# One fused block on one Trainium2 core: the same ramp, another hand-written order from the first value products on, the gate row for w_out among the first output projections, the last output tile in two parts

## The chip, the core and the metric

The kernel runs on one core of a Trainium2 chip. A core has five engines that each run their own list of instructions in order: TensorE (PE, matrix products, with PEld for the loading of weights), VectorE (DVE), ScalarE (ACT), GpSimd (POOL) and SyncE (SP, which only issues DMAs here). They meet through semaphores. The metric is device time in microseconds (us) of one execution; times of a kernel are given as the median of several runs.

## What is computed

x has S = 2048 rows and D = 448 columns, in bf16. Cut to what matters:

```python
mod = (silu(c) @ w_mod)                      # six vectors sa, ca, ga, sb, cb, gb
h = layernorm(x) * (1 + ca) + sa
q, k, v = split(h @ wqkv)                    # 16 heads of 28
phi(u) = concat(softmax(u @ w_phi), softmax(-u @ w_phi))
kv, z = phi(k)^T v, sum(phi(k))              # per head
x = x + ga * ((phi(q) kv / (phi(q) z)) @ wo)
h = layernorm(x) * (1 + cb) + sb
z = gelu(h @ w_in)                           # 2048 x 1792
z1, z2 = z[:, :896], layernorm(z[:, 896:])
g = w_sp @ z2 + b_sp                         # w_sp is 2048 x 2048
x = x + gb * ((z1 * g) @ w_out)
```

## The kernel before

The rows are cut into 16 tiles of 128. All weights and activations stay in SBUF; modulation is folded into the weights (SC and SH steps scale and shift them, so that the layer norm's scale and offset cost nothing per tile), and the gates ga and gb are folded into wo and w_out (gr and ge make a gate row with one product and one copy, wos and wts multiply it in).

Everything is written as small steps, and one string, `ORDER`, names the steps in the order in which they are emitted. A word is `step:arguments@bank/engine`. A loop at the end of `fast_path` runs over the words; each engine gets its instructions in this order, and no scheduler moves them (`tc.manual_schedule()`). The letter behind the slash says which engine does the step: V is VectorE, S ScalarE, G GpSimd, Y SyncE. The part behind the @ is the PSUM space: A0, A1 and A2 have two banks each, B0 and B1 one bank each. A step that takes a space waits until what stood there has been read. So the order of the words sets the order on every engine, and where two engines must meet.

The steps of which this text speaks, by place in the program:

- Start: `consts` (L682) fills constants, f_zero among them; `du` (L726) are dummy products of f_zero that fill PE ahead of the first data; `ld` (L679) issues a load; `l1s`, `l1e`, `l1r`, `l1a` (L855 to L867) are the first layer norm, `l1a` its last step per tile; `X` (L877) transposes the first tiles on PE, `T1` (L872) the others two at a time with a DMA on SP.
- Attention, first half: `EPq` (L796) folds w_phi into the q weights; `kM`, `vM`, `qM` (L890, L898, L945) are the products for k, v and q; `kE` and `kF` (L893) the exponentials of plus and minus k on ScalarE, `vC` (L901) the copy of v, `kS`, `kR`, `kP` (L904 to L911) sums, reciprocals and products that make the softmax; `kA` (L921) adds a tile to kv. `qE` and `qF` (L950) are the exponentials of q.
- Attention, second half: `nM` (L973) numerator and denominator, `nX`, `nC`, `nS`, `nT` (L977 to L989) the division, `T2` (SP) a transpose, `wM` (L1003, L1005) the output projection into x_ps, `wR` and `wQ` (L1010, L1012, L1017) the residual add and the square for the second layer norm, `l2R`, `l2r`, `l2a` the rest of it. `nA` and `l2a` write tiles for the transposes `T2` and `T3`.
- gMLP: `SCw` (L796, L798, L800) scales w_in; `zM` (L1049) is the second half of h @ w_in, `zG` (L1053) its gelu on ScalarE, `zQ`, `zR`, `zW`, `zN` its layer norm, which ends in the tile z2n (L1072); `yM` and `yG` (L1078, L1081) are the first half.
- Spatial product: `W` (L1086) are transposing loads of pieces of w_sp on SP, into the buffers f_wsp, f_Eq and f_hT; the last two are buffers of earlier stages, and so such a load waits until the earlier stage has read them. The product is arranged in blocks with seven products in place of eight: `gM` (L1145) is one plain column of blocks, `P` (L1124) the others, `d` and `x` (L1133, L1140) their sums and the product with z1, `tT` (L1102) and `sS` (L1109) sums of tiles of z2n and of w_sp.
- Output: `oM` (L1159), `oE` (L1162), `oD` (L1165): seven matmuls, the eviction with the residual add, and the store of one tile.

`general_path` is a fallback that a flag starts; it does not run here.

Of the kernel before, what the change touches and what calls it, by code (L numbers as in the profile page):

```python
# [481 lines left out]
ORDER = """tbl du:8@B1 m2b/V ld:wk/Y du:3@A2 m2a/V du:11@A1 ld:c/Y ct@B0 ld:x1/S l1s:1 ld:x0/S l1s:0 m1/G ld:phi/Y ce:1 m3 FTk:1@B1 ce:2 l1e:1,2/G ld:wsa/Y du:2@A0  # L482
l1e:0,1/G FTk:0@A0 ld:wca/Y ce:3 ce:4 bd/V ld:x2/Y ld:wq/Y l1r:0,1 l1a:0/V du:6@A2 X:0@B0 ETk:0/S csA@A2 ETk:1/V PFk:2@B1 l1r:1,2 esA l1a:1/G X:1@A0 XE:0/V
m4 du:2@A2 FSk@B0 ccA@A1 FCk/S PFk:0@B0 ecA XE:1/S EPk:0/V EPk:2/S l1s:3 du:1@A2 PFk:1@A1 EPk:1/S ld:wv/Y l1s:2 PFk:3@A0 l1e:2,4/V EPk:3/S du:2@B0 kM:1@B1
FTq:1@A2 ETq:1/V ld:x3/Y FTq:0@B0 ETq:0/V kM:0@A0 kF:1 FSq@A2 FCq/V kE:1 kS:1 PFq:1@B0 scb kF:0 kE:0 l1r:2,4 l1a:2/G l1a:3/G l1s:4 X:2@B1 SHv@A1 PFq:2@A2
# [4 lines left out]
qF:0 kS:5 vC:6 kM:6@A2 l1a:10/G kS:4 vC:5 l1a:11/G qM:2@A1 kF:6 kR:5 kF:7 kR:4 kE:6 kP:5/V ld:wcb/Y qF:2 T1:8,10 kP:4/V kS:6 kR:6 vM:7@B1 kE:7 T1:10,12  # L490
kA:3@A0 wos:0/G l1e:12,16/G vM:4@A2 l1r:12,16 vC:7 qE:2 l1a:15/G kM:9@B0 kF:9 l1a:12/V l1a:14/G kM:8@B1 l1a:13/V vM:9@A1 kE:9 kS:7 kR:7 kF:8 vC:4 kS:9
kE:8 kS:8 T1:12,14 kM:10@B0 kP:6/G kE:10 kP:7/G kR:8 kF:10 kA:4@A0 kA:5@A0 kM:11@B1 kE:11 T1:14,16 kS:10 vM:10@B0 kF:11 kS:11 kA:6@A0 vC:9 kA:7@A0 kM:12@B1
kP:8/G kR:10 kE:12 kR:9 kP:9/V kR:11 vC:10 kP:10/V kF:12 kS:12 kM:13@A1 kR:12 vM:8@A2 kM:15@B0 vC:8 kF:13 kP:11/G kM:14@B1 ld:wsb/Y kE:13 kS:13 kR:13 kE:14
W:0,6 kF:14 kE:15 kA:8@A0 kA:9@A0 kP:12/V kS:14 vM:11@A1 kF:15 kS:15 kA:10@A0 vM:14@B1 kR:14 vC:11 vM:15@B0 vC:14 vM:12@A2 vM:13@B1 vC:12 kA:11@A0 vC:13
kP:13/G kA:12@A0 kR:15 kP:14/V kP:15/V wos:2/V kA:13@A0 kA:14@A0 vC:15 kA:15@A0 KV:0/V KV:1/V KZ:0 ld:win0/S qM:3@A2 KZ:1 nM:0@A1 qE:3 ld:wout/S nM:1@A0
nX:0 nX:1 qF:3 nC:0 csB@B0 W:0,1 ld:win1/Y nC:1 nS:0 ccB@B1 nT:0 qM:4@A2 qE:4 nA:0/V nT:1 ecB nA:1/V wos:3/V qM:5@A1 nM:2@A0 qF:4 esB nX:2 nM:3@A2 nX:3
FB@B1 wos:1/V nC:2 qE:5 T2:0,1 nC:3 nS:1 FBc/S qF:5 nT:2 nA:2/G wM:0/S@B0 nT:3 SHw:3@B1 wR:0/S SCw:0,3/S T2:1,2 nM:5@A1 nX:5 nM:4@A0 nC:5 nX:4 nC:4 nA:3/V
wQ:0/S wM:1/S@B0 wR:1/S SHw:2@B1 SCw:2,1/S qM:6@A2 SCw:0,0/S SCw:3,1/G nS:2 nT:5 nT:4 T2:2,4 nM:6@A1 wQ:1/V qE:6 nX:6 nM:7@A0 nA:5/G nA:4/V nX:7 SCw:0,2/S
qF:6 nC:6 nC:7 nS:3 nT:7 wM:2/S@B0 wR:2/S wM:3/S@B1 wR:3/S qM:7@A2 wQ:2/S nT:6 wQ:3/S nA:6/V SCw:1,1/V SCw:1,0/V nM:9@A0 T2:4,6 qE:7 nM:8@A1 wM:5/S@B1
nX:8 nX:9 wM:4/V@B0 l2R:0,2/G l2r:0,2 l2a:0/G T3:0,1 l2a:1/V qF:7 nC:8 wR:5/S zM:0@A2 gt nA:7/G l2R:2,4/G nC:9 nS:4 nT:9 nT:8 zG:0 l2r:2,4 l2a:3/G T2:6,8  # L500
wR:4/V l2a:2/G nM:10@A0 T3:1,2 T3:2,4 wQ:5/S nX:10 nA:8/V SCw:3,0/G wM:6/V@B1 wR:6/V nM:11@A1 wQ:4/S nX:11 nA:9/V SCw:2,0/V l2R:4,6/G zM:1@A2 nC:11 nC:10
zG:1 l2r:4,6 nS:5 l2a:5/V wQ:6/S wM:7/V@B1 l2a:4/G yM:0,0@B0 zM:2@A2 yG:0,0 T2:8,10 nT:10 wR:7/V zQ:1/V T3:4,6 W:1,3 zM:3@A0 zG:2 wM:8/V@A2 wQ:7/S l2R:6,8/G
W:0,5 wM:9/V@B1 nT:11 nA:11/V nA:10/V zG:3 wR:8/V zQ:0/S nM:12@A0 nM:13@A2 l2r:6,8 l2a:6/G zM:4@A1 wR:9/V nX:13 nX:12 T2:10,12 zR:0,2/G zQ:3/S wQ:8/S W:1,7
yM:0,4@B0 zG:4 yM:0,1@B1 zQ:4/S nC:13 nM:15@A1 nC:12 zW:0,2 nX:15 yG:0,1 nS:6 nT:13 wQ:9/S nM:14@A2 nX:14 l2a:7/G nT:12 zN:0/V zM:5@A0 yG:0,4 T3:6,8 l2R:8,10/G
l2r:8,10 nA:12/V l2a:9/G nA:13/V nC:15 wM:11/V@B1 zG:5 nC:14 nS:7 l2a:8/G nT:14 zQ:5/S wR:11/V yM:0,5@B0 nT:15 yM:1,3@A0 T2:12,14 yM:1,0@A2 nA:14/G zQ:2/V
nA:15/V yG:0,5 zR:4,6/G zN:1/G wM:10/V@B0 zW:4,6 wM:13/V@A1 wM:12/V@B1 wR:13/V W:2,0 W:0,2 zN:5/G yG:1,0 yG:1,3 yM:1,4@A0 wR:12/V zR:2,4/V zW:2,4 zN:3/G
zN:2/V zM:6@A2 wQ:12/S yM:1,5@B1 wQ:13/S wR:10/V wQ:10/V zG:6 zM:7@A1 T2:14,16 W:2,6 wQ:11/S l2R:10,12/G l2R:12,14/V l2r:10,12 wM:15/V@B0 yG:1,5 zN:4/V
l2a:11/V yM:0,2@A2 wR:15/V zQ:6/S T3:8,10 yM:0,3@B1 W:1,4 W:0,0 zG:7 l2r:12,14 yM:1,1@A1 l2a:13/G yG:1,4 W:0,4 l2a:10/V T3:10,12 yG:1,1 yM:1,2@A0 l2a:12/V
wM:14/V@B0 yG:1,2 zQ:7/V zM:8@A1 yG:0,2 T3:12,14 wR:14/V wQ:14/V yG:0,3 zG:8 wQ:15/V l2R:14,16/V zQ:8/S zR:6,8/G zW:6,8 zN:7/G zM:9@A2 zG:9 zN:6/V l2r:14,16
W:1,1 yM:1,6@B1 yM:0,6@A1 yG:0,6 yG:1,6 zQ:9/V l2a:15/V zM:11@A0 yM:2,5@B0 zM:10@A1 l2a:14/V zG:11 guard@B1 zQ:11/V zG:10 zQ:10/S zM:12@A0 yM:2,4@B1 W:1,5  # L510
zR:8,10/G W:1,0 zG:12 zM:13@A2 zW:8,10 T3:14,16 zR:10,12/G zW:10,12 yG:2,5 yM:3,6@A0 zN:8/V yG:2,4 zN:9/V zG:13 yM:2,2@B1 yG:2,2 yG:3,6 zM:15@A1 yM:3,4@A2
W:1,2 W:2,2 zN:10/V zG:15 zQ:15/S zM:14@A0 zQ:13/V yG:3,4 zN:11/G zG:14 zQ:12/V zR:12,14/V yM:2,6@B0 yM:3,0@A2 yM:3,1@B1 W:1,6 yG:2,6 zQ:14/S tT:1,2/G
yG:3,0 yM:3,2@A0 yM:2,0@A1 zW:12,14 sS:0,1,0,8/V yM:2,1@B0 yM:2,3@A2 yG:3,2 yM:3,5@A0 tT:1,0/V yG:2,0 yG:3,1 zR:14,16/G zW:14,16 zN:14/V zN:15/V yM:3,3@A1
# [4 lines left out]
P:1,0,1 d:1,0,2 P:0,2,2 tT:4,1/V read P:0,2,5 W:3,6 W:2,5 W:3,7 P:0,1,7 d:0,2,4 wts:5/V W:3,3 P:1,1,1 d:0,2,5 wts:6/V P:0,2,3 x:0,2,4/G d:0,2,7 sS:1,1,0,8/V
yG:2,1 sS:1,2,0,8/V d:0,2,6 gM:3@B0 d:0,1,7 gG:3 P:0,1,4 P:0,2,4 x:0,2,7/V x:0,1,7/G d:0,1,8 x:0,2,6/V oM:0,0,7@B0 x:0,1,8/G oE:0 oD:0/Y oM:1,0,7@B1 d:1,1,1
P:1,0,6 d:1,0,1 oE:1 d:1,0,3 d:1,1,2 oM:3,0,7@B0 P:1,0,5 P:1,1,6 oE:3 sS:1,3,0,8/G P:1,0,7 oD:1/Y d:0,2,8 d:1,0,5 d:1,0,7 gM:2@B1 gG:2 P:1,0,2 P:1,1,2  # L520
oM:2,0,7@B1 P:1,0,4 x:1,0,7/V x:0,2,8/G d:1,0,4 P:1,2,1 x:1,0,4/G oM:5,0,7@B0 d:1,1,3 sS:1,4,0,8/V P:1,1,5 d:1,1,5 oE:5 oD:5/Y P:1,1,7 oE:2 d:1,0,8 P:1,0,3
oM:4,0,7@B0 d:1,1,7 d:1,0,6 x:1,0,6/G oD:2/Y d:1,2,1 P:1,2,6 oD:3/Y d:1,2,2 P:1,2,2 oM:6,0,7@B1 P:1,2,7 x:1,0,8/V d:1,2,3 oE:6 P:1,1,3 d:1,1,6 P:1,2,5
oE:4 oD:4/Y oD:6/Y x:1,1,7/G P:1,1,4 x:1,1,6/G oM:7,0,7@B0 d:1,1,4 x:1,1,4/G d:1,2,4 x:1,2,4/G hint d:1,2,5 P:1,2,3 d:1,2,7 d:1,2,6 oE:7 x:1,2,6/G P:1,2,4
d:1,2,8,256,512 oD:7/Y oM:9,0,7@B0 oE:9 oD:9/Y d:1,2,8,0,256 oM:8,0,7@B1 oE:8 x:1,2,7/G oD:8/Y oM:10,0,7@B0 d:1,1,8 oE:10 x:1,1,8/G oD:10/Y oM:11,0,7@B1
oE:11 oD:11/Y x:1,2,8,0,256/G oM:12,0,7@B0 oE:12 oD:12/Y oM:13,0,7@B1 oE:13 oD:13/Y x:1,2,8,256,512/G oM:14,0,7@B0 oM:15,0,7@B1 oE:14 oD:14/Y oE:15 oD:15/Y
# [741 lines left out]
```

## Time and profile before

| | |
|---|---|
| time, median of 3 runs | 249.26 us (248.95 to 249.69) |
| profiled execution | 249.4 us |
| its span | 247.6 us |
| instructions | 4188 |
| PE busy | 240.5 us, 97% |
| DVE busy | 182.5 us, 74% |
| ACT busy | 104.8 us, 42% |
| POOL busy | 116.3 us, 47% |

The span is the time between the first and the last instruction that the profiler saw; the profiled execution's own time has some 1.8 us more around it. PE's share of 97% counts a matmul from its start to its modelled end. Rows of the timeline have the start, the length, the engine, the line and the operation, with output and inputs by the program's names; a bracket at the end holds the idle time before it and what ended it. Rows with x2 or more are several instructions put together. SPq and ACTq are the DMAs that SP and ACT issue, with the time of the issue.

### The profile page before, as it was taken

The numbers are of one execution on the slowest core, as the hardware profiler recorded it, in microseconds if no ns is written. First come the engines' busy times: TensorE is split into PE (matmuls) and PEld (weight loads), VectorE is DVE, ScalarE is ACT, GpSimd is POOL, SyncE is SP. The second block draws the span as 40 slices with busy tenths as digits, with TensorE's granted clock in tenths as the row PEclk, the third lists the DMA queues.
The fourth block names the chain that finished last, engine by engine and source line by source line (L and its number), as shares of the span: only waits on it lengthen the run. The fifth ranks groups of instructions, "written<-read, shape, count | busy, mean of one in ns | idle before, by whom it ended". The sixth has DMA issues, their size and how long they took to land.

```text
span 247.6 us, 4188 instructions
## 1 busy us (share of the span) xinstructions
PE 240.5 (97%) x1533; PEld 126.8 (51%) x1533; DVE 182.5 (74%) x369; ACT 104.8 (42%) x217; POOL 116.3 (47%) x175
## 2 busy tenths in 40 slices
...
GB/s 178 293 217 102 193 86 177 194 113 178 51 72 110 127 162 136 163 158 176 179 177 0 162 181 173 0 1 0 3 0 37 0 0 3 56 0 37 21 95 65
DMA packets 68207, 25.22 MB, mean 102 GB/s; under 512 B 58129, under 2 KB 67602, under 8 KB 68178
## 3 DMA queue, kind: packets, MB, share of 16 engines
...
q8 instruction: 14, 0.23, 0.4%
...
## 4 chain that ended last, share of the span: by engine, by line
PE 85%; POOL 6%; ACT 3%; DVE 2%; DMA 1%; issue 1%; POOLq 0%
PE g_ps L1124 29%; PE o_ps L1159 9%; PE z_ps L1049 7%; PE q_ps L945 6%; PE k_ps L890 5%; PE v_ps L898 5%; PE g_ps L1145 5%; PE z_ps L1078 4%; PE x_ps L1005 4%; PE kvacc L921 3%; PE warm_ps L729 3%; PE num L973 2%; POOL f_zv L1035 1%; DMA f_hT<-f_xpad 1%; DVE f_z2n L1072 1%
## 5 line engine op out<-in xcount | busy, mean ns | idle before, releaser
L1133 DVE TENSOR_TENSOR f_zb<-g_ps,f_zb 128x512 f32<-128x512 f32 (+1 forms) x31 | 20.5, 670 | 17.1 <-PE g_ps L1124 16.7
L1124 PEld LDWEIGHTS <-f_z2n 128*128 128x128 bf16 x192 | 18.8, 98 | 22.7 <-issue 0.3
L1140 POOL TENSOR_TENSOR f_z1T<-f_zb,f_z1T 128x512 bf16<-128x512 f32 (+1 forms) x11 | 12.0, 1102 | 33.6 <-DVE f_zb L1133 33.6
L1049 PE MATMUL z_ps<-f_ar,f_hT 112*128 112x448 bf16 (+1 forms) x128 | 26.6, 352 | 0.0
L1140 POOL TENSOR_TENSOR f_z1T<-f_Sx,f_z1T 128x512 bf16<-128x512 f32 x6 | 8.0, 1332 | 39.3 <-DVE f_Sx L1133 39.3
L1078 PE MATMUL z_ps<-f_hT,f_ar 112*128 112x512 bf16 x112 | 26.1, 379 | 0.0
L1159 PE MATMUL o_ps<-f_wout,f_z1T 128*128 128x448 bf16 x112 | 22.5, 352 | 0.0
L1124 PE MATMUL g_ps<-f_ar 128*128 128x512 bf16 x96 | 22.4, 379 | 0.0
L1081 ACT ACTIVATE f_z1T<-z_ps,f_zb 128x512 bf16<-128x512 f32 x28 | 18.2, 684 | 5.2 <-PE z_ps L1078 5.1
L950 ACT ACTIVATE f_Eq<-q_ps 112x1024 bf16<-112x1024 f32 x16 | 16.3, 1032 | 5.8 <-PE q_ps L945 5.8
L1049 PEld LDWEIGHTS <-f_hT 112*128 112x128 bf16 (+1 forms) x128 | 12.2, 97 | 11.6
L1078 PEld LDWEIGHTS <-f_ar 112*128 112x128 bf16 x112 | 11.0, 98 | 12.6
L893 ACT ACTIVATE f_E<-k_ps 128x448 bf16<-128x448 f32 x32 | 15.8, 555 | 3.8 <-PE k_ps L890 3.7
L989 DVE TENSOR_TENSOR f_ar<-num,f_w 128x896 bf16<-128x896 f32 x16 | 17.0, 1087 | 0.4
L904 DVE TENSOR_REDUCE f_ksum<-f_E 128x32 f32<-128x896 bf16 x16 | 16.9, 1064 | 0.5 <-ACT f_E L893 0.4
L1124 PE MATMUL g_ps<-f_Eq,f_z2n 128*128 128x512 bf16 x72 | 16.5, 379 | 0.0
L1159 PEld LDWEIGHTS <-f_z1T 128*128 128x128 bf16 x112 | 11.0, 98 | 10.7
L1053 ACT ACTIVATE f_zb<-z_ps 128x896 bf16<-128x896 f32 x16 | 14.6, 913 | 4.1 <-PE z_ps L1049 3.8
L1162 DVE TENSOR_TENSOR f_xpad<-o_ps,f_x 128x448 bf16<-128x448 f32 x16 | 9.9, 622 | 8.0 <-PE o_ps L1159 7.9
L945 PE MATMUL q_ps<-f_hT,f_Wq 113*128 113x512 bf16 (+1 forms) x64 | 15.0, 379 | 0.6 <-ACT f_Eq L950 0.6
L1124 PEld LDWEIGHTS <-f_ar 128*128 128x128 bf16 x96 | 9.4, 98 | 11.1 <-DVE f_ar L1102 0.2
L1005 PE MATMUL x_ps<-f_ar 112*128 112x448 bf16 x64 | 14.1, 352 | 0.3 <-DVE f_x L1012 0.3
...
## 6 DMA issues: line engine op xcount, KB each, us to landing
out_dram<-f_xpad SPq DMA_DIRECT2D x16, 112.0 KB, 1.7
...
f_wmg<-in_w_mod_dram SPq DMA_DIRECT2D x2, 392.0 KB, 9.9
f_ar<-in_B_w_in_dram SPq DMA_DIRECT2D x1, 784.0 KB, 5.6
f_ar<-in_B_w_in_dram ACTq DMA_DIRECT2D x1, 784.0 KB, 5.4
f_wout<-in_B_w_out_dram ACTq DMA_DIRECT2D x1, 784.0 KB, 5.6
...
```

The lines of the kernel that those rows point to most:

```text
L904: nc.vector.tensor_reduce(out=ksum[:, i], in_=Er[i % NR][:].rearrange("p s (c f h) -> p (s c) h f", c=4, h=HP), axis=AX.X, op=ALU.add)
L945: nc.tensor.matmul(t[:, u, :], lhsT=Wq[0:KR[m], m, cc * CB:cc * CB + P], rhs=hT[0:KR[m], 4 * st:4 * st + 4, m, :], start=(m == 0), stop=(m ...
L950: nc.scalar.activation(out=Eq[st // 2][0:CB, 2 * c2:2 * c2 + 2, s, (st % 2) * 512:(st % 2 + 1) * 512], in_=ps["q" + str(n)][0:CB, :, :], f ...
L989: nc.vector.tensor_tensor(out=tr[i % 2][:], in0=numv(i)[:, :, :, 0:DH], in1=wr[i // 2 % 2][:, i % 2].unsqueeze(3).to_broadcast([P, 2, H, D ...
L1005: nc.tensor.matmul(t[:, 0, 0:D], lhsT=oT[0:CB, i % 4, cc, :], rhs=wo_s[0:CB, cc, :], start=(cc == 0 and not with_x), stop=(cc == KC - 1))
L1049: nc.tensor.matmul(t[:, hf, 0:D], lhsT=hT[0:KR[m], i, m, :], rhs=win_s[0:KR[m], m, FH + hf * D:FH + (hf + 1) * D], start=(m == 0), stop=(m ...
L1078: nc.tensor.matmul(t[:, 0, :], lhsT=win_s[0:CB, m, fc * P:(fc + 1) * P], rhs=hT[0:CB, 4 * st:4 * st + 4, m, :], start=(m == 0), stop=(m == ...
L1081: nc.scalar.activation(out=stage_b()["z1T"][:, fc, st * 512:(st + 1) * 512], in_=ps["y%d_%d" % (st, fc)][:, 0, :], func=ACT.Gelu_apprx_tan ...
L1124: nc.tensor.matmul(g, lhsT=sta[:, m, :], rhs=mov[:, m, :], start=(m == 0 and i in (1, 6, 7)), stop=(m == 7), skip_group_check=True)
L1133: nc.vector.tensor_tensor(out=o, in0=x, in1=y, op=ALU.add)
L1140: eng.tensor_tensor(out=z, in0=T[r][:, c0:c1], in1=z, op=ALU.mult)
L1159: nc.tensor.matmul(ps["o" + str(t)][:, 0, 0:D], lhsT=later["z1T"][:, FO[n], t * P:(t + 1) * P], rhs=wout_s[:, FO[n], :], start=(n == 0), s ...
```

## The change

The words for the ramp are the same: the first 102 words of `ORDER` stand as they were. From the first value product (vM:2) on, the same steps are emitted in another order, until gM:3; from there to the last tile but one the words are as before again. What is moved:

- Loads: win1 (the half of w_in for z1) stands on ScalarE's queue right behind EPq:2 (before: SP's, behind the first two loads of w_sp); wmga follows x4, x5 moves to SP's queue, wo to ScalarE's behind kE:4, and wmgb, win0, wcb and wout come together later.
- gr:1 and ge:1, the gate row for w_out, move from the second value products to behind qM:6, among the first output projections.
- Several steps change engine, SCw:1,0 from V to S, zQ:1 and zQ:2 from V to S, tT:1,2 from G to V, nA:1, l2a:1 and l2a:5 from V to G among them.
- yM:2,1 moves from before gM:1 to behind gM:0.
- W:3,5 and the loads behind it keep their order, but f_hT, into which W:3,5 writes, is read by yM:2,1.

In the constants, f_zero is filled first and for 256 of its 512 columns (the dummies read no more). The last output tile, 15, is made in two parts: columns 0 to 255 in B1 and 256 to 447 in B0, each with its own seven matmuls, eviction and store; the first store goes on ScalarE's queue, the second on SP's. Because the string stands on one line now, line numbers behind it are 43 smaller (L1086 becomes L1043), from the new functions on 32 smaller.

The three places at which instructions move that the prediction speaks of. First ScalarE's list at the first value products (f_Wq is EPq, f_vaug vC, f_E kE or kF, f_Eq qE). Before:

```order
L796 ACTIVATE f_Wq<-pf_ps,f_ca_136 113x448
L796 ACTIVATE f_Wq<-pf_ps,f_ca_136 112x448
L901 CAST f_vaug<-v_ps 128x16x28
L893 ACTIVATE f_E_125<-k_ps 128x448
L796 ACTIVATE f_Wq<-pf_ps,f_ca_136 112x448
L893 ACTIVATE f_E_125<-k_ps 128x448
L661 DMA f_x<-in_A_x_dram 128x4x448
```

and with the change:

```order
L753 ACTIVATE f_Wq<-pf_ps,f_ca_136 113x448
L753 ACTIVATE f_Wq<-pf_ps,f_ca_136 112x448
L602 DMA f_ar<-in_B_w_in_dram 112x2x1792
L850 ACTIVATE f_E_125<-k_ps 128x448
L858 CAST f_vaug<-v_ps 128x16x28
L753 ACTIVATE f_Wq<-pf_ps,f_ca_136 112x448
L850 ACTIVATE f_E_126<-k_ps 128x448 x2
```

The load of w_in's half stands here now, behind the second f_Wq, and the load of x is gone to SP.

Second, ScalarE between the first two gelus of z2 (f_zb from z_ps is zG, f_ar from f_x is wQ, f_Sx is nX). Before:

```order
L1053 ACTIVATE f_zb,f_zs_92<-z_ps 128x896
L1017 ACTIVATE f_ar,f_s_89<-f_x 128x448
L977 COPY f_Sx<-num 128x32
L1017 ACTIVATE f_ar,f_s_89<-f_x 128x448
L977 COPY f_Sx<-num 128x32
L1053 ACTIVATE f_zb,f_zs_92<-z_ps 128x896
```

and with the change:

```order
L1010 ACTIVATE f_zb,f_zs_92<-z_ps 128x896
L934 COPY f_Sx<-num 128x32
L753 ACTIVATE f_ar<-f_ar,f_cb_83 112x896
L934 COPY f_Sx<-num 128x32
L974 ACTIVATE f_ar,f_s_89<-f_x 128x448 x2
L1010 ACTIVATE f_zb,f_zs_92<-z_ps 128x896
```

One scaling of w_in (SCw:1,0) has come in between.

Third, GpSimd at the end of z2's layer norm (f_zm and f_zv are mean and variance, L1035 the power that makes the reciprocal root). Before:

```order
L1072 TENSOR_SCALAR f_z2n<-f_zb,f_zm,f_zv 128x896
L1102 TENSOR_TENSOR f_ar<-f_z2n 128x1024
L1035 TENSOR_TENSOR f_zv<-f_zv,f_mhalf 128x2
L1025 TENSOR_SCALAR f_zm<-f_zs_92 128x2
L1026 TENSOR_TENSOR f_sq<-f_zm 128x2
L1028 TENSOR_SCALAR f_zv<-f_zs_93 128x2
L1029 TENSOR_TENSOR f_zv<-f_zv,f_sq 128x2
L1032 TENSOR_SCALAR f_zv<-f_zv 128x2
L1035 TENSOR_TENSOR f_zv<-f_zv,f_mhalf 128x2
L1072 TENSOR_SCALAR f_z2n<-f_zb,f_zm,f_zv 128x896
```

and with the change:

```order
L992 TENSOR_TENSOR f_zv<-f_zv,f_mhalf 128x2
L1029 TENSOR_SCALAR f_z2n<-f_zb,f_zm,f_zv 128x896 x2
L982 TENSOR_SCALAR f_zm<-f_zs_92 128x2
L983 TENSOR_TENSOR f_sq<-f_zm 128x2
L985 TENSOR_SCALAR f_zv<-f_zs_93 128x2
L986 TENSOR_TENSOR f_zv<-f_zv,f_sq 128x2
L989 TENSOR_SCALAR f_zv<-f_zv 128x2
L992 TENSOR_TENSOR f_zv<-f_zv,f_mhalf 128x2
L1029 TENSOR_SCALAR f_z2n<-f_zb,f_zm,f_zv 128x896
L1059 TENSOR_TENSOR f_xpad<-f_z2n,f_ar 128x1024
```

The sum of z2n tiles (L1102, tT:1,2) no longer stands between the statistics; it is on VectorE.

The diff, cut to its core, with the parts of the string of which this text speaks:

```diff
-EPq:2/S vC:2 ld:wmgb/Y kE:2 PFq:3@A0 EPq:3/S ld:wmga/Y l1s:8 kM:3@A2 kF:2 qM:1@A1 kR:1 ld:x5/S l1r:4,8 vM:0@B1 kR:0 kS:2 kE:3 kF:3 vM:1@A2 l1s:10 qE:1
-l1a:4/G gr:1@A0 vC:0 l1s:13 l1a:5/G vC:1 ge:1 gr:0@B1 l1a:7/G kS:3 l1a:6/G vC:3 T1:4,6 kP:0/G T1:6,8 qF:1 kR:2 ge:0 qM:0@A2 qE:0 kP:1/G l1s:12 kM:5@B0
-kM:4@B1 kF:4 kP:2/V vM:5@A1 kA:0@A0
...
+EPq:2/S vM:2@A1 l1e:4,8/G l1r:4,8 ld:win1/S ld:wmga/Y kM:3@A0 l1a:4/G PFq:3@B0 vM:3@A2 kE:2 vC:2 kS:0 EPq:3/S ld:x5/Y kF:3 qM:1@A1 l1s:8 kE:3 vC:3 kF:2 vM:1@A2 kR:0 qF:1 vM:0@B1 vC:1 l1s:10 gr:0@A0 l1a:5/G qM:0@A2 kS:2 vC:0 l1a:7/G l1a:6/G kS:3 kP:0/G ge:0 kR:1 qE:1 kA:0@A0 T1:4,6 l1s:11 kR:2 qF:0 kM:5@A1 kM:4@B1
...
+qM:6@A2 SCw:2,1/S nT:4 wR:1/S nA:4/V gr:1@B0 qE:6 nM:7@A0 ge:1
...
-zG:0 l2r:2,4 l2a:3/G T2:6,8 wR:4/V l2a:2/G nM:10@A0 T3:1,2 T3:2,4 wQ:5/S nX:10 nA:8/V SCw:3,0/G wM:6/V@B1 wR:6/V nM:11@A1 wQ:4/S nX:11 nA:9/V SCw:2,0/V l2R:4,6/G zM:1@A2 nC:11 nC:10 zG:1
+zG:0 wM:6/V@B1 wR:6/V nX:10 nC:10 wR:4/V nM:11@A1 SCw:1,0/S zM:1@A2 nX:11 SCw:3,0/G wQ:5/S wM:7/V@B1 T3:2,4 yM:0,0@B0 nC:11 nS:5 wQ:4/S zG:1
...
-yM:2,1@B0 yM:2,3@A2 yG:3,2 yM:3,5@A0 tT:1,0/V yG:2,0 yG:3,1 zR:14,16/G zW:14,16 zN:14/V zN:15/V yM:3,3@A1 yG:3,5 zN:13/G tT:1,1/V yG:3,3 zN:12/V
+zR:14,16/G tT:1,0/V zW:14,16 yM:3,3@A1 zN:15/V yG:3,3 zN:14/V yG:3,2 yM:2,3@B0 yG:2,3 zN:11/G tT:2,0/V tT:4,0/G gM:1@B1 gG:1 tT:1,2/V
...
+gM:0@B1 P:0,0,2 gG:0 yM:2,1@B0 tT:1,1/V W:3,4 P:0,0,7 W:3,5
...
-oM:14,0,7@B0 oM:15,0,7@B1 oE:14 oD:14/Y oE:15 oD:15/Y
+oM:14,0,7@B0 oP:15,0,256@B1 oE:14 oD:14/Y oP:15,256,448@B0 oF:15,0,256 oG:15,0,256/S oF:15,256,448 oG:15,256,448/Y
...
     def consts():
+        nc.vector.memset(zero[:, 0:256], 0.0)
         nc.gpsimd.memset(wk_raw[0:CB, :, D:D + 16], 0.0)
         nc.gpsimd.memset(wq_raw[0:CB, :, D:D + 16], 0.0)
         nc.vector.memset(one1[:], 1.0)
         nc.vector.memset(warm[:], 0.0)
-        nc.vector.memset(zero[:], 0.0)
...
+    def oP(t, a, b, slot):
+        o = ps["op" + str(a)] = bank(slot, "o_ps")
+        for n in range(FC):
+            nc.tensor.matmul(o[:, 0, 0:b - a], lhsT=later["z1T"][:, FO[n], t * P:(t + 1) * P], rhs=wout_s[:, FO[n], a:b], start=(n == 0), stop=(n == FC - 1))
+
+    def oF(t, a, b):
+        nc.vector.tensor_tensor(out=later["ot"][t % 4][:, a:b], in0=ps["op" + str(a)][:, 0, 0:b - a], in1=x_sb[:, t, a:b], op=ALU.add)
+
+    def oG(t, a, b, eng):
+        eng.dma_start(out=outv[t][:, a:b], in_=later["ot"][t % 4][:, a:b])
```

46 lines of the change are left out of this document (3 added, 43 removed).

## The prediction, before the result was known

> **What bounds the kernel now.** I read the page's engine shares and chain first, then TensorE's waits, then the end of the timeline.
>
> ```profile
> span 247.6 us, 4188 instructions
> PE 240.5 (97%) x1533; PEld 126.8 (51%) x1533; DVE 182.5 (74%) x369; ACT 104.8 (42%) x217; POOL 116.3 (47%) x175
> PE 85%; POOL 6%; ACT 3%; DVE 2%; DMA 1%; issue 1%; POOLq 0%
> ```
>
> PE (TensorE) works for 240.5 of 247.6 us, and the chain that ended last is PE for 85%. The change takes no matmul away, so it can only win what PE stands still, and what lies behind its last matmul. PE's waits are five:
>
> ```profile
> PE warm_ps L729 <- DVE f_zero L687: 1.2, 1, 1.2
> PE q_ps L945 <- ACT f_Eq L950: 0.6, 1, 0.6
> PE x_ps L1005 <- DVE f_x L1012: 0.3, 1, 0.3
> PE g_ps L1145 <- DVE f_z2n L1072: 0.2, 1, 0.2
> PE warm_ps L729 <- DVE f_Wk L800: 0.2, 1, 0.2
> ```
>
> The columns are the sum, the number and the longest wait. Together they are 2.5 us; behind them lies the tail, which starts when the last eviction can:
>
> ```profile
> 243.17 0.62 DVE L1162 TENSOR_TENSOR f_xpad<-o_ps,f_x 128x448 bf16<-128x448 f32 x1 [0.70 <-PE o_ps L1159]
> ```
>
> From 243.17 to 247.6 there are 4.4 us: eviction, one store, end. So nearly 7 us are not matmul, of which the edits touch the waits at f_zero, f_x and f_z2n and the eviction, and between them PE can only be slowed. Every new order must keep PE as dense as the old one was.
>
> **The parts, in order of time.** The sum is made against the profiled execution, 249.4 us (span 247.6 and 1.8 around it), which is 0.1 over the median of 249.26; the same difference is then taken off the median.
>
> *Start.* VectorE's memset of f_zero comes first and fills half as much.
>
> ```profile
> 0.90 0.27 DVE L687 MEMSET f_zero<- 128x256 uint32 x1
> 8.65 0.71 POOL L867 TENSOR_SCALAR f_xpad<-f_x,f_nm,f_rs 128x448 bf16<-128x448 bf16 x1
> 9.42 0.40 PE L880 MATMUL xt_ps<-f_ident,f_xpad 128*128 128x128 bf16 x4
> ```
>
> Half of 0.27 and the two small memsets ahead of it are some 0.25 us by which PE can begin its dummies sooner. But X:1 starts at 9.42, just behind POOL's l1a:1, which ends at 9.36 and hangs on x's load and its statistics, not on PE. PE then waits there instead. Value 0, bounds -0.25 (if the rest of the head is PE's own) and 0.
>
> *Loads at the first value products.* win1 (half of w_in, 784 KB) goes from SP's queue, where it stood behind the first w_sp loads, to ScalarE's, behind EPq:2, the second of the two in the first row here, which ends at 17.60 + 1.21 = 18.8. It is in flight with wmga, x5 and the transposes T1:4,6 that kM:5 needs.
>
> ```profile
> 17.60 1.21 ACT L796 ACTIVATE f_Wq<-pf_ps,f_ca 113x448 bf16<-113x448 f32 x2
> 22.75 2.73 SPq L872 DMA_TRANSPOSE f_hT<-f_xpad  x2
> DMA to landing us min/median/max: 3.1/3.2/3.3
> 23.32 1.68 PE L956 MATMUL gr_ps<-f_wmg,f_scb 112*128 112x448 bf16 x8
> 24.84 1.90 PE L945 MATMUL q_ps<-f_hT,f_Wq 113*128 113x512 bf16 x8
> 26.57 1.68 PE L890 MATMUL k_ps<-f_Wk,f_hT 113*128 113x448 bf16 x8
> f_ar<-in_B_w_in_dram ACTq DMA_DIRECT2D x1, 784.0 KB, 5.4
> f_wmg<-in_w_mod_dram SPq DMA_DIRECT2D x2, 392.0 KB, 9.9
> 24.08 3.34 POOL L911 TENSOR_TENSOR f_phik<-f_E,f_kr 128x896 bf16<-128x896 bf16 x2
> ```
>
> T1:4,6, issued at 22.75, lands at 26.05 by the longest of 3.3. gr:1 leaves this place; gr:0 and gr:1 took 24.84 - 23.32 = 1.52, one of them 0.76, so qM:0 starts at 24.08. It takes 26.57 - 24.84 = 1.73, and kA:0, now ahead of kM:5, some 0.42: PE reaches kM:5 at 26.23, not 26.57. The cover shrinks from 0.5 to 0.2. kA:0 needs POOL's first multiply, which starts at 24.08 and takes half of 3.34, so ends at 25.75, against PE's 25.81: a tie. win1 lands by its own 5.4 at 24.2, before the transposes do. I take +0.1: bounds 0 (T1 as before), and what T1 loses if win1 needs the 9.9 us that the wmg loads needed: 18.8 + 9.9 = 28.7, PE at 26.23, so +2.4.
>
> *The gate row gr:1* stands behind qM:6 now. Its four matmuls still cost PE 0.76, once: 0. ScalarE's extra copy ge:1 there is one of 0.53 in a stretch where the x_ps evictions and the q exponentials tie with PE; bounds 0 and +0.2, taken 0, since it is placed behind qE:6 and not before it.
>
> *ScalarE between the first two z2 gelus.* SCw:1,0 moves from VectorE to ScalarE, between zG:0 and zG:1.
>
> ```profile
> 66.62 1.97 ACT L796 ACTIVATE f_ar<-f_ar,f_cb 112x896 bf16<-112x896 bf16 x2
> 80.39 0.92 ACT L1053 ACTIVATE f_zb<-z_ps 128x896 bf16<-128x896 f32 x1 [0.45 <-PE z_ps L1049]
> 81.81 2.45 PE L1049 MATMUL z_ps<-f_ar,f_hT 113*128 113x448 bf16 x12
> ```
>
> One SCw is half of 1.97, so 0.98; 0.45 of idle time takes it up, and zG:1 comes 0.53 late: from 80.92 to 81.84. zM:2 reuses zG:1's bank (A2) and stands at 81.81. With the step from one engine to the other, some 0.1 as between rows above (9.36 to 9.42), that is +0.13; bounds 0 and +0.25.
>
> *wM:15.* Before, VectorE reached the residual add that frees its bank last.
>
> ```profile
> 98.73 0.62 DVE L1012 SCALAR_TENSOR_TENSOR f_x<-x_ps,f_x 128x448 bf16<-128x448 f32 x1
> 103.04 0.62 DVE L1012 SCALAR_TENSOR_TENSOR f_x<-x_ps,f_x 128x448 bf16<-128x448 f32 x1
> 103.72 0.92 PE L1005 MATMUL x_ps<-f_ar 112*128 112x448 bf16 x4 [0.26 <-DVE f_x L1012]
> ```
>
> Now wR:10 is first of its group, at about 98 to 99, and wM:15 comes four us later: -0.26 (bounds -0.26 and 0, the latter if a later step hangs on the same adds).
>
> *gM:1.* The wait is for the last z2n tiles, whose POOL statistics stand behind one 2.12 us sum.
>
> ```profile
> 130.11 2.12 POOL L1102 TENSOR_TENSOR f_ar<-f_z2n 128x1024 bf16<-128x1024 bf16 x1 [7.34 <-ACT f_ar L1017]
> 135.07 1.71 DVE L1072 TENSOR_SCALAR f_z2n<-f_zb,f_zm,f_zv 128x896 bf16<-128x896 bf16 x2 [6.42 <-POOL f_zv L1035]
> 137.31 0.50 DVE L1072 TENSOR_SCALAR f_z2n<-f_zb,f_zm,f_zv 128x896 bf16<-128x896 bf16 x1
> 134.87 2.75 PE L1145 MATMUL g_ps<-f_Eq,f_z2n 128*128 128x512 bf16 x12
> 137.87 1.04 PE L1145 MATMUL g_ps<-f_Eq,f_z2n 128*128 128x512 bf16 x4 [0.24 <-DVE f_z2n L1072]
> ```
>
> That sum (tT:1,2) goes to VectorE behind gM:1, so the last z2n tile comes up to 2.1 earlier, near 136. yM:2,1 leaves from before gM:1, which starts some 0.9 sooner (four matmuls of 512 columns, 3.62/16 = 0.23 each by the sixteen quoted next) and has done twelve of its matmuls at 134.87 - 0.9 + 2.75 = 136.7, the place of the old wait: no wait, -0.24 (bounds -0.24, and +0.6 if the new z2n order, with two tiles more on POOL at 1.1 each, is late by so much).
>
> *w_sp's queue.* W:3,5 overwrites what yM:2,1 reads. Before, yM:2,1 ran ahead of gM:1; now it stands behind gM:0 and one product more. Behind W:3,5 on SP stand twelve loads.
>
> ```profile
> 147.37 3.62 PE L1124 MATMUL g_ps<-f_ar 128*128 128x512 bf16 x16
> 150.12 2.61 SPq L1086 DMA_TRANSPOSE f_hT<-in_B_w_sp_dram  x2
> DMA to landing us min/median/max: 3.4/4.2/5.0
> 175.15 2.28 DVE L1109 TENSOR_TENSOR f_ar<-f_hT 128x4096 bf16<-128x4096 bf16 x1
> ```
>
> gM:0 ended, and these sixteen began, at 147.37. Less 0.9 and the wait of 0.24, plus a product (half of 3.62) and yM:2,1, that is 148.9. At half of 2.61 an issue the last load goes at 148.9 + 12 x 1.31 = 164.6 and lands at 168.8 (median 4.2), while its reader starts at 175.15. That cover of 6.3 hides the delay: 0, and if each issue took 0.5 more it would be gone.
>
> *Tail.* The last tile's eviction and store are two, of 256 and 192 columns; the second is all that stands behind the last matmul.
>
> ```profile
> L1133 DVE TENSOR_TENSOR f_zb<-g_ps,f_zb 128x512 f32<-128x512 f32 x29 | 19.7, 687 | 16.6 <-PE g_ps L1124 16.2
> L1133 DVE TENSOR_TENSOR f_zb<-g_ps,f_zb 128x256 f32<-128x256 f32 x2 | 0.8, 420 | 0.5 <-PE g_ps L1124 0.5
> out_dram<-f_xpad SPq DMA_DIRECT2D x16, 112.0 KB, 1.7
> q1 hardware_dynamic: 864, 0.69, 21.5%
> ```
>
> A column is (687 - 420)/256 = 1.04 ns, so 448 columns give 620, as the row at 243.17 has it, and 192 give 353 ns: -0.27. The seven more matmuls stream the same columns in all. The store shrinks from 112 to 48 KB, but what ends it is mostly not bytes: 16 stores of 112 KB take 1.7 us each alone. Taken -0.25; bounds -0.35 (if the bytes count) and +0.1 (if the two stores hinder each other).
>
> [...] The second part's rows have 192 x 2 = 384 B (the old ones 896). [...]
>
> qM:4's wait of 0.58 keeps its neighbours and stays. Sum: +0.10 + 0.13 - 0.26 - 0.24 - 0.25 = **-0.52**: 248.9 on the profiled execution, **248.7** on the median.
>
> **Rivals.**
>
> *win1 holds up T1:4,6.* For it: the cover is 0.2, and the wmg loads show 9.9 us from issue to landing. Against it: 5.4 us for the other half of w_in, as large and on this queue, when less else was in flight. At the full price kM:5 waits 2.4, not 0.1: 248.74 + 2.3 = 251.0. Slower by over 0.3% (0.75 us, about what can be told from no change here) from a stall of 1.4 on, T1:4,6 landing after 27.6.
>
> *The w_sp queue is late.* With 0.5 more per issue the cover is used up; a stall of 0.5 to 1.2 before gM:3 gives 249.2 to 249.9. Against it: the issues of 1.31 are steady.
>
> *All of it comes.* The start gives its 0.25, T1 and zG:1 cost nothing: -0.25 - 0.26 - 0.24 - 0.27 = -1.0: 248.2. For it: each of the two costs rests on a tie of 0.1.
>
> *The freed waits come back elsewhere.* VectorE is busy for 74% and runs in order; steps that changed engine (nA, zQ, wQ) make new ties in a PE that was dense by a balanced order. One or two of 0.25 eat the two waits: 249.3.
>
> [...]
>
> **How the numbers follow.** The forecast, 248.7, has 0.46 (own range 248.3 to 249.2); all of it comes 0.20; win1 holds up T1 0.14; freed waits come back 0.09; w_sp late 0.06; short rows 0.05. Range: at the top the win1 case reaches from 249.9 to 251.0, I cut it at 250.4; at the bottom 247.9 takes in the third case and a tail gain of 0.35. Faster by over 0.3% (under 248.51): 0.20 from the third case and 0.10 from the forecast's lower part: 0.30. Slower (over 250.0): 0.13 from win1, 0.09 from a new wait as in the w_sp or the ties' case with a larger price: 0.22. Within: 0.48.
>
> **What would show it.** PE's waits of the changed kernel: f_x at x_ps and f_z2n at g_ps gone, f_Eq at q_ps still 0.6, a small one for zG:1's bank at z_ps. kM:5 starting by 26.4, T1:4,6 landing by 26.2. win1 to landing under 6 us. Last eviction 0.35 and its end to span's end no longer than before. The start's wait near 1.0, and another of 0.2 ahead of X:1. A wait of over 1 us for f_hT at k_ps, or one at gM:3, would make the forecast wrong.

## The result: slower by 1.2%

The change takes 252.49 us (252.13 to 253.23, 4 runs), the kernel before beside it 249.47 (248.95 to 250.62, 4 runs): a ratio of 1.0118, interval 1.0073 to 1.0163. Timed a second time it was 251.71 against 249.29, 1.0107 (1.0068 to 1.0146); why the first timing is 0.8 longer stays open. The forecast was 248.7, range 247.9 to 250.4.

The profiled execution took 252.82 us with a span of 250.3, so 2.5 lie around it, not 1.8. The page's first two lines:

```profile
span 250.3 us, 4211 instructions
PE 240.8 (96%) x1540; PEld 127.4 (51%) x1540; DVE 180.1 (72%) x363; ACT 109.5 (44%) x224; POOL 124.4 (50%) x173
```

and all of PE's waits:

```profile
PE k_ps L847 <- DMA f_hT<-f_xpad: 1.8, 1, 1.8
PE xt_ps L837 <- DVE f_xpad L824: 1.1, 1, 1.1
PE warm_ps L686 <- DVE f_warm L644: 1.0, 1, 1.0
PE q_ps L902 <- ACT f_Eq L907: 0.6, 1, 0.6
```

The waits at x_ps (f_x) and g_ps (f_z2n) are gone, as forecast. Two new ones are larger than both: 1.8 us for a transposed tile f_hT, and 1.1 in the head. Beside the kernel before, step for step, PE is 1.11 us late from kM:0 on, 3.15 after the f_hT wait, 2.27 at its last matmul; between these it wins 0.88, for the most part in the places of the old waits. From PE's last matmul to the end of the span it is 4.87 us (4.45 before), and 0.73 more lies around. 2.27 + 0.42 + 0.73 is the 3.4 us between the two profiled executions.

**The f_hT wait.** The timeline of the changed kernel; first the rows of SP, then PE's:

```profile
36.45 1.34 SPq L1043 DMA_TRANSPOSE f_wsp<-in_B_w_sp_dram  x1
37.88 0.54 SPq L609 DMA_DIRECT2D f_wm<-in_w_mod_dram  x1
38.52 4.21 SPq L829 DMA_TRANSPOSE f_hT<-f_xpad  x2
...
45.43 1.32 PE L847 MATMUL k_ps<-f_Wk,f_hT 113*128 113x448 bf16 x6 [1.83 <-DMA f_hT<-f_xpad]
```

The same place before, where PE does not wait:

```profile
36.51 2.61 SPq L872 DMA_TRANSPOSE f_hT<-f_xpad  x2
39.17 0.57 SPq L652 DMA_DIRECT2D f_wm<-in_w_mod_dram  x1
39.80 3.88 SPq L1086 DMA_TRANSPOSE f_wsp<-in_B_w_sp_dram  x2
...
42.29 1.68 PE L890 MATMUL k_ps<-f_Wk,f_hT 113*128 113x448 bf16 x8
```

The steps T1:12,14 and T1:14,16 stood ahead of a w_mod load (wsb) and of the w_sp loads; now W:0,5 and wsb stand ahead of them. The list of moved loads in the section on the change does not have these two. What the two transposes took from issue to landing, in the change and then before:

```profile
DMA to landing us min/median/max: 6.2/6.5/6.9
```

```profile
DMA to landing us min/median/max: 3.5/3.6/3.7
```

So T1:12,14 was issued 2.0 us later and took 3.1 more: it landed at 45.38, and kM:12 had been due at 43.6.

**The head.** The changed kernel's timeline, PE:

```profile
1.04 4.05 PE L686 MATMUL warm_ps<-f_zero 128*128 128x256 bf16 x22 [1.04 <-DVE f_warm L644]
8.53 0.40 PE L837 MATMUL xt_ps<-f_ident,f_xpad 128*128 128x128 bf16 x4 [1.10 <-DVE f_xpad L824]
12.38 1.70 PE L847 MATMUL k_ps<-f_Wk,f_hT 113*128 113x448 bf16 x4
```

and two of its stretches, in which the third number from the end is the granted clock of PE:

```profile
11.00:14.50 3.50, 3.50 (x27) 2.55 (x25) 2.38 (x8) 2.26 (x5) 0.70 (x1) 0.52 1.12 328
14.50:18.00 3.50, 3.50 (x57) 2.79 (x55) 2.87 (x6) 2.72 (x7) 2.23 (x4) 1.00 0.65 186
```

The same row of the timeline and the first stretch, before:

```profile
12.10 1.04 PE L890 MATMUL k_ps<-f_Wk,f_hT 113*128 113x448 bf16 x4
```

```profile
11.00:14.50 3.50, 3.27 (x38) 2.35 (x35) 3.27 (x10) 2.72 (x6) 0.79 (x2) 1.00 1.12 324
```

The data still sets the place: X:0 starts at 8.53 in both, and PE now stands still ahead of it for 1.10 us, until VectorE has made its tile. The prediction had a wait for the data too, but ahead of X:1. What it had not: from 10.93 to 14.34 us, for 3.41 us, PE has half its clock (granted 0.50), and kM:1's four matmuls take 1.70 us, not 1.04. I call this stretch the lost head. The 22 first dummies took 4.05 us, not 4.88: from the one at 4.16 us on they follow each other at 0.11 us, not at 0.21. The trace's record of the granted clock begins with this, at 4.10 us and at 1.00 (before: at 6.69 us, behind the last of the 22); below, the doubling is this moment. So PE ran out of dummies early.

**The tail.** The changed kernel's timeline, and the answer on its DMA issues from 244 us on (KB each, us to landing):

```profile
244.00 0.62 DVE L1119 TENSOR_TENSOR f_xpad<-o_ps,f_x 128x448 bf16<-128x448 f32 x1 [0.70 <-PE o_ps L1116]
245.45 0.36 DVE L1130 TENSOR_TENSOR f_xpad<-o_ps,f_x 128x192 bf16<-128x192 f32 x1 [0.26 <-PE o_ps L1127]
```

```profile
out_dram<-f_xpad ACTq DMA_DIRECT2D x1, 64.0 KB, 3.4
out_dram<-f_xpad SPq DMA_DIRECT2D x1, 48.0 KB, 2.9
```

The last eviction is 0.36, the 353 ns that the row's slope gave. But its store of 48 KB takes 2.9 us to land; the 112 KB of before took 2.2.

### The profile page after: what moved, and what is told of

It reads as the page before. It is cut to its first block, busy times and chain, and to the rows that moved or that the text cites. A ratio compares the mean times of both kernels' runs of the same rounds, so it can differ in the third digit from the quotient of the medians.

```text
span 250.3 us, 4211 instructions
## 1 busy us (share of the span) xinstructions
PE 240.8 (96%) x1540; PEld 127.4 (51%) x1540; DVE 180.1 (72%) x363; ACT 109.5 (44%) x224; POOL 124.4 (50%) x173
## 4 chain that ended last, share of the span: by engine, by line
PE 82%; DVE 7%; DMA 4%; POOL 3%; ACT 1%; issue 0%; POOLq 0%
PE g_ps L1081 29%; PE z_ps L1006 10%; PE z_ps L1035 10%; PE o_ps L1116 8%; PE g_ps L1102 6%; PE x_ps L962 5%; PE q_ps L902 4%; DVE f_st L813 3%; DMA f_hT<-f_xpad 3%; PE num L930 2%; PE k_ps L847 2%; DVE f_ksum L861 2%; POOL f_xpad L824 2%; DMA f_x<-in_A_x_dram 2%; PE v_ps L855 2%; PE kvacc L878 1%
## 5 line engine op out<-in xcount | busy, mean ns | idle before, releaser
L1035 PE MATMUL z_ps<-f_hT,f_ar 112*128 112x512 bf16 x112 | 26.1, 379 | 0.0
L1006 PE MATMUL z_ps<-f_ar,f_hT 112*128 112x448 bf16 (+1 forms) x128 | 26.0, 352 | 0.0
L1097 POOL TENSOR_TENSOR f_z1T<-f_Sx,f_z1T 128x512 bf16<-128x512 f32 x6 | 9.1, 1510 | 27.8 <-DVE f_Sx L1090 27.8
L1116 PE MATMUL o_ps<-f_wout,f_z1T 128*128 128x448 bf16 x105 | 21.2, 352 | 0.0
L1035 PEld LDWEIGHTS <-f_ar 112*128 112x128 bf16 x112 | 10.9, 98 | 12.5
L847 PE MATMUL k_ps<-f_Wk,f_hT 113*128 113x448 bf16 (+1 forms) x64 | 15.1, 367 | 1.8 <-DMA f_hT<-f_xpad 1.8
L1116 PEld LDWEIGHTS <-f_z1T 128*128 128x128 bf16 x105 | 10.3, 98 | 10.0
L1119 DVE TENSOR_TENSOR f_xpad<-o_ps,f_x 128x448 bf16<-128x448 f32 x15 | 9.2, 622 | 7.3 <-PE o_ps L1116 7.2
```

The costliest lines, as they stand in the source:

```text
L847: nc.tensor.matmul(t[:, 0, 0:D], lhsT=hT[0:KR[m], i, m, :], rhs=Wk[0:KR[m], m, :], start=(m == 0), stop=(m == KC - 1))
L1006: nc.tensor.matmul(t[:, hf, 0:D], lhsT=hT[0:KR[m], i, m, :], rhs=win_s[0:KR[m], m, FH + hf * D:FH + (hf + 1) * D], start=(m == 0), stop=(m ...
L1035: nc.tensor.matmul(t[:, 0, :], lhsT=win_s[0:CB, m, fc * P:(fc + 1) * P], rhs=hT[0:CB, 4 * st:4 * st + 4, m, :], start=(m == 0), stop=(m == ...
L1097: eng.tensor_tensor(out=z, in0=T[r][:, c0:c1], in1=z, op=ALU.mult)
L1116: nc.tensor.matmul(ps["o" + str(t)][:, 0, 0:D], lhsT=later["z1T"][:, FO[n], t * P:(t + 1) * P], rhs=wout_s[:, FO[n], :], start=(n == 0), s ...
```

## The experiments

Ratios are to the kernel before, timed beside each set.

### The head: is it the memset?

The change with the old memset:

```diff
-        nc.vector.memset(zero[:, 0:256], 0.0)
         nc.gpsimd.memset(wk_raw[0:CB, :, D:D + 16], 0.0)
...
         nc.vector.memset(warm[:], 0.0)
+        nc.vector.memset(zero[:], 0.0)
```

> The changed kernel with f_zero filled as before (512 columns, last of the five constants). Theory C (clock): the early start made PE run out of dummies, it stood still for 1.10 us ahead of X:0 (7.43 to 8.53), and the clock that this cost is why kM:1 and what follows ran at half pace up to 14.9 us; kM:0 starts at 14.91 in the changed kernel, 13.80 before. With the old fill there is no idle stretch over 0.3 us ahead of X:0, kM:0 starts at 13.8 to 13.9, and the time falls by 1.0 to 1.2 us, to about 251.4. Rival D (data): the head is late because x came 0.19 us later (first statistics at 4.97, not 4.78); then kM:0 stays near 14.9 and the time changes by less than 0.3 us.

And the reverse edit in the kernel before:

> The kernel before, with only the fill of f_zero halved and put first. Theory C: PE starts at 1.04, stands still for about 1.1 us ahead of X:0, the granted clock of the first 15 us falls from 1.00 to about 0.9, kM:0 starts near 14.9 and the time is 0.9 to 1.2 us longer than before. Rival D: nothing over 0.3 us.

The first took 251.44 us, 1.0093 (1.0063 to 1.0123); its profiled execution had a whole head (kM:0 at 13.90), but beside 251.71 for the change itself this is 0.3 less, not 1.0. The second took 249.58, 1.0009 (0.9993 to 1.0025), though its profiled execution had the lost head in full (PE idle for 1.08, kM:0 at 14.96). Neither theory held. The executions tell why: beside these sets the kernel before ran 145 times, 106 times up to 249.76 us and 39 times from 250.04 on, with none between. The mean granted clock of each execution goes with it: 0.993 or less in 35 of the 39, 0.995 or more in all of the 106. (The other four of the 39 kept the clock, so something else made them long; in two profiles PE waits for a later f_hT transpose, for 1.3 us with the new memset alone and 1.0 in the run with W:0,5 ahead.) With the old memset, too, two of the nine other kernels' profiled executions had lost the head. So it is a matter of the single execution. Counted by that clock, 28 of 83 executions with the new memset lost the head and 59 of 241 with the old one: a third against a quarter, a difference that is not clear of chance. Of the change's first four executions two had lost it, of its second six three, so this does not explain the 0.8 us between its two timings; the executions with a whole head differ as much (252.13 and 252.15 against 251.16 to 251.51), and the runs do not say why.

In all profiles the sign is when the doubling comes: at 4.0 to 4.4 us in the six with a lost head, during the first 22 dummies; at about 5.0 us or later in the others, where PE then idles ahead of X:0 for 0.70 us at most. Four more dummies ahead of X:0 should take the second group away:

```diff
-l1a:0/V du:6@A2 X:0@B0
+l1a:0/V du:10@A2 X:0@B0
```

> The kernel before with four more dummy products (ten for six, 0.43 us at full clock) ahead of X:0. In the profiles taken so far PE idled ahead of X:0 for 0.86 to 1.26 us in the six with a slow kM:1 and for 0 to 0.70 in the twelve without. Theory C: with 0.43 us more cover the idle stretch is under 0.8 always, the clock does not fall, and the upper group of executions (1.2 us longer, about a quarter) is gone: all but an odd one of 12 between 248.8 and 249.7. Rival: the groups have another cause, and a fifth to a third of the executions stay at 250.0 to 250.9. In the lower group, where idle was 0 to 0.4, X:0 may come up to 0.3 later.

> The order alone with the same four more dummies. Theory C: 248.2 to 248.7, no execution over 249.2. Rival: median 248.9 and a third over 249.2, as without them.

In the kernel before: 249.49 (249.14 to 250.21, 12 runs), 0.9987 (0.9961 to 1.0013): no execution at 250.3 or more, where 32 of the 145 lay. All twelve kept the clock (0.995 or more in the mean), the three at 250.0 to 250.2 too, but they are some 0.1 us longer than the executions of the kernel before that kept it; X:0 stands 0.2 later in the profile. So the loss of the head is gone, but four of the twelve are over the 249.7 that was expected, and the median is no better. In the new order without the change's other parts (below): 248.68 (248.25 to 249.09), all twelve within 0.8 us and at a clock of 0.997 or more, where 10 of 24 without the dummies were over 249.2 (seven of these at 0.992 or less). In the traces the doubling lies 3.0 to 5.5 us behind the first dummy (3.06 in the change, 5.46 before), and in the six profiles with a lost head the granted clock then stood at 1.00 for 6.83 us, ahead of the 3.41 us at 0.50. Why the moment varies from one execution to the next, no run shows. The shortest idle stretch ahead of X:0 that went with the half clock was 0.86 us, the longest that did not 0.70.

### The f_hT wait

The change with both transposes moved ahead:

```diff
-W:0,5 kM:11@B0 kS:10 ld:wsb/Y kF:11 kR:9 kE:11 T1:12,14 kS:11 T1:14,16 kA:5@A0
+kM:11@B0 kS:10 kF:11 kR:9 kE:11 T1:12,14 kS:11 T1:14,16 W:0,5 ld:wsb/Y kA:5@A0
```

> The changed kernel with the transposes T1:12,14 and T1:14,16 moved on SP's queue ahead of the w_sp load W:0,5 and the w_mod load wsb, nothing else. Theory Q (queue and company): T1:12,14 needs its last input at 37.1, was issued at 38.52 behind these two, and took 6.9 us to landing beside them, where it took 3.7 before; moved ahead it is issued near 37.1 and lands by 41.5, kM:12 no longer waits 1.83 us, and the time falls by 1.8 to 2.0 us, to about 250.6. Rival P (producers): the late step is GpSimd's l1a:13, 0.6 later than before; then kM:12 still waits over 1 us and the time falls by less than 0.8.

249.90 us, 1.0027 (1.0002 to 1.0052): 1.8 less than the change's second timing. T1:12,14 went out at 36.14 and landed at 39.88; the wait is gone. The producer rival fell. Which of the two loads it is, was asked in both ways, first with wsb left ahead, then with W:0,5 left ahead:

> The changed kernel with only the w_sp load W:0,5 moved behind T1:12,14 and T1:14,16 on SyncE's queue; the w_mod load wsb stays ahead of them. In the run with both moved T1:12,14 took 3.7 us to landing, in the change 6.9. If the transposing load W:0,5 is the one that holds it up: 3.7 to 4.5, no wait at kM:12, time as with both moved. If it is wsb: 5.5 or more to landing, though issued 1.3 earlier; kM:12's wait is then 0 to 1.

> The changed kernel with only the w_mod load wsb moved behind T1:12,14 and T1:14,16; the w_sp load W:0,5 stays ahead of them. With W:0,5 alone moved T1:12,14 still took 7.0 us from issue to landing. If wsb holds it up: 3.7 to 4.5 us, no wait at kM:12, time as with both moved (249.9, lower group 249.2 to 249.9). If either of the two is enough: 5.5 us or more, a wait of 1 us or more at kM:12, 251 or more.

Both took 250.10 us (1.0017, 0.9987 to 1.0046; and 1.0023, 0.9997 to 1.0049). The transposes' landing with wsb ahead, then with W:0,5 ahead:

```profile
DMA to landing us min/median/max: 6.5/6.8/7.0
```

```profile
DMA to landing us min/median/max: 5.2/5.4/5.6
```

Either load is enough to hold the transposes up; what the single moves win is the earlier issue (36.06 and 36.98, not 38.52), which leaves kM:12 a wait of 0.58 and none. So the wait of 1 us or more and the 251 that were expected for this second case did not come. What the three traces have in common: T1:12,14 lands 2.1 to 2.4 us after the load that was issued just ahead of it on SP's queue (42.96 to 45.38 in the change, 40.85 to 43.06 and 40.49 to 42.61 here). With no load in flight ahead it takes 3.7 from its issue. Whether the place in the queue does this or the load's packets on the DMA engines, is not shown: no run had such a load on another queue.

### The tail

The change with the last tile as before:

```diff
-oM:14,0,7@B0 oP:15,0,256@B1 oE:14 oD:14/Y oP:15,256,448@B0 oF:15,0,256 oG:15,0,256/S oF:15,256,448 oG:15,256,448/Y
+oM:14,0,7@B0 oM:15,0,7@B1 oE:14 oD:14/Y oE:15 oD:15/Y
```

> The changed kernel with the last output tile in one piece as before. Theory T (stores): from PE's last matmul to the end of the span it took 4.89 us with two parts and 4.46 before, because the second store's 384-byte rows and the other two stores in flight take 2.9 us to landing against 2.2, and 0.7 us more lies around the span (2.5, not 1.8) because a second queue has a store to finish; undone, the tail is 4.4 to 4.5 again, what lies around the span 1.8 to 1.9, and the time falls by 0.4 to 1.1 us. Rival of my prediction (the eviction counts): the time rises by 0.25 us.

250.42 us, 1.0042 (1.002 to 1.0064): 1.3 less than the change's second timing, and 1.8 around the span again. The tail alone, put into the kernel before, and there too the same with one store of whole rows behind both evictions:

> The kernel before, with only the last output tile in two parts, as the change has it. Theory T: the tail within the span 4.8 to 4.9 (before 4.45), 2.3 to 2.6 around the span (before 1.8), the time 0.9 to 1.3 longer, about 250.4. My prediction's term: -0.25, 249.1.

> The kernel before, with the last tile's matmuls and evictions in two parts, but one store of whole rows behind both, on SyncE's queue as before. If the two stores (their queue, number or short rows) were the loss and the shorter eviction a gain: tail within the span 4.1 to 4.3, 1.8 around, time 0.2 to 0.3 shorter, about 249.0. If the split of matmuls and evictions itself costs: 0.3 longer or more.

The first took 251.40 us (1.0088, 1.0055 to 1.0122), the second 250.68 (1.0053, 1.0035 to 1.0070). (Three of the first's six executions had lost the head; the other three took 250.80 to 251.28.) So neither the second store nor the short rows are the main loss, and theory T fell: the split itself costs. What it changes on PE is a wait. The second part writes into B0, which is free only when tile 14 is evicted; before, PE's last wait was for tile 13. Behind it PE's list ends with a branch over the fallback. The trace has one record of it in each kernel; before, in the change, in the last experiment (two evictions, one store):

```profile
L1234 PEldq COMPARE_BRANCH  x1: 4031/4031/4031, 241.2 to 241.2; - x1
```

```profile
L1202 PEldq COMPARE_BRANCH  x1: 3814/3814/3814, 244.7 to 244.7; - x1
```

```profile
L1245 PEldq COMPARE_BRANCH  x1: 3754/3754/3754, 242.5 to 242.5; - x1
```

It takes some 3.8 us, and starts 1.9 us ahead of PE's last matmul's end before, 0.7 ahead with the split. The other engines' branches take 0.05 to 0.08. To try it, the two parts, still in the kernel before, got banks of the block products that are long free (`later["G"][0]` and `[1]`), so that PE's last wait is the one of tile 14's own bank:

```diff
-oP:15,0,256@B1 oE:14 oD:14/Y oP:15,256,448@B0
+oP:15,0,256@G0 oE:14 oD:14/Y oP:15,256,448@G1
```

> The kernel before with the last tile in two parts and two stores, as the change has it, but the parts' matmuls write into two PSUM banks of the block products that have been free for 4 us, not into B1 and B0. Theory W (PE's last wait): PE's list ends with a branch to the program's end; its record starts right behind PE's last wait (241.22 before, 242.49 to 244.69 with the new tail, whose second part waits for the eviction of tile 14), a 16 KB instruction fetch starts 1.02 us later in every run, and the branch ends 3.4 to 4.0 us after it began; from its start to the end of the execution it took 7.6 to 8.3 us in every run. With free banks the last wait is tile 14's, some 1.2 us earlier than before: the two-part tail then costs nothing, 249.0 to 249.4, or gains up to 0.3. Theory T (two stores, short rows): still 1 to 2 us longer than before.

> As the run before, but with one store of whole rows behind both evictions. Theory W: 249.0, 0.3 less than before and 1.3 to 1.7 less than the same in B1 and B0 (250.68). Theory T or a cost of the seven more matmuls: 250.4 to 250.7 again.

> The kernel before with the last tile in one piece as it was, only its matmuls in a free bank of the block products. Theory W, if the branch sets the end before too: the branch starts 1.3 us earlier and the time falls, by at most the 0.6 or so by which the branch's end, not the last store, is late; if the store sets it, no change, 249.3. A longer time speaks against theory W.

With two stores 249.73 (0.9994, 0.9970 to 1.0019), with one 249.59 (1.0001, 0.9973 to 1.0029): the banks alone take 1.7 and 1.1 us off. Only the banks differ, and with them PE's last wait: the late wait is the cause. It does not act through PE's matmuls: with two stores the last one ends at 244.45 with free banks and at 244.52 without (both profiles with a lost head), and with one store the store goes out at 243.59 and 243.63. The loss lies behind that. Theory W's gain on top is not there. The last tile whole in a free bank took 250.00 (1.0013, 0.9988 to 1.0038), not less, so an earlier branch is not simply better. How the late wait costs is read from the traces. Their instruction fetches of 16 KB (on queue q8, which the page lists as instruction), with the branch and the last store, in us:

```
                          branch  fetch 1  branch end  fetch 2  last store (issue, landing)  around the span
before                    241.22  242.23   245.25      246.01   243.83 246.05                1.81
the change                244.69  245.71   248.50      249.28   245.83 248.77                2.54
two parts, one store      242.49  243.50   246.24      247.03   243.63 246.35                2.87
two parts, free banks     242.21  243.23   246.16      246.93   244.87 247.21                1.98
one store, free banks     240.93  241.94   244.82      246.10   243.59 245.88                2.00
whole tile, free bank     240.02  241.04   244.01      244.78   243.91 246.98                1.90
```

The first fetch starts 1.01 to 1.02 us behind the branch in each, the second 0.8 to 1.3 behind its end. The last store took 2.2 to 2.3 us where no such fetch ran in its first two microseconds, and 2.7 to 3.1 where one did (the first fetch in the change and in the row below it, the second in the last row). All twenty traces of this case divide much the same way: 1.9 to 2.5 us where no such fetch ran for more than 0.1 us in the store's first 1.8 us, 2.6 to 3.2 where one did. That the fetches hold up the stores, and that a late branch is what lies around the span, fits all six rows but was not tried by itself: a kernel without the branch would be another program. What holds PE's branch for 3.8 us, and why the same branch takes the other engines under 0.1 us, no run shows.

### The order alone, and the change mended

The new order with the old memset, the old tail, and the two transposes ahead of W:0,5 and wsb; timed twice:

> The changed order alone: f_zero and the last tile as before, and T1:12,14 and T1:14,16 ahead of W:0,5 and wsb. By the theory of three terms what is left are the waits that the new order does away with (0.42 at wM:15, 0.29 at gM:1, 0.17 at one block product): -0.9, lower group at 248.3, median about 248.5. Rival: the order has other losses that the three terms hide; then it is 249.3 or more.

> The order alone once more, beside the two before it: 248.4 to 249.0, if the 0.4 us gain of the first time holds.

248.87 us, 0.9974 (0.9952 to 0.9996), and 248.95, 0.9964 (0.9941 to 0.9988). Its profiled execution has PE's last matmul end 1.09 us earlier than before.

With the split tail in free banks and one store, beside the second of these:

> The order alone (f_zero as before, both transposes ahead of W:0,5 and wsb) with the last tile in two parts in free PSUM banks and one store. The order alone gave 248.87 (ratio 0.9974), the tail in this form 249.59 beside 249.41 (1.0001). Theory W in its plain form (the earlier branch is free and the shorter eviction counts): 248.5 to 248.7. By the runs with free banks, which gained nothing over the old tail: 248.8 to 249.1.

248.95 us, 0.9978 (0.9952 to 1.0004): the shorter eviction adds nothing. Then the change itself with only two mends, wsb behind the transposes and free banks for the last tile:

> The whole change with two mends only: wsb behind the two transposes, and the last tile's two parts in free PSUM banks, both its stores kept, f_zero filled as in the change. By the terms measured (kM:12 -1.9, tail -1.0 to -2.0 of the change's 252): 248.6 to 249.3, not distinguishable from or faster than the kernel before. If the head's early start is a loss of its own in the mean: 249.3 to 250.

248.86 us, 0.9967 (0.9942 to 0.9991). So the two losses account for the whole of the change's 1.2%, and without them it gains 0.3%. The lowest median of all is the order alone with four more dummies: 248.68, 0.9958 (0.9936 to 0.9979); the intervals of these kernels overlap.

The change once more, beside the tail's experiments, is the second timing given at the top:

> The whole change once more, beside the others of this set. In the runs so far executions of every kernel, the one before among them, fall into two groups some 1.2 us apart, as PE's clock does or does not fall to half ahead of kM:1; the four of the changed kernel were then mostly in the upper one. Theory (three terms): lower group at 249.2 + 1.9 (kM:12) + 1.0 (tail) - 0.9 (waits gone) = 251.2, upper at 252.3, median 251.2 to 252.3. Rival (the head is lost in every execution of the changed kernel): all at 252.1 or more.

The first theory held there (251.16 to 253.66, four of six under 252.0).

## Why the prediction was wrong

*Loads at the first value products* (+0.1 taken, 0 to +2.4): wrong place. At T1:4,6 nothing was lost: it was issued at 23.87 and landed at 27.22, kM:5 followed at 27.37 without a wait. The sign that the prediction named for being wrong, a wait of over 1 us for f_hT at k_ps, did come, but at kM:12. The rival was a load on ScalarE's queue that slows the transposes; what happened was two loads ahead of them on SP's own queue, so that its price (2.4 named, 1.83 measured) came near is luck. The step that failed is the list of moved loads: win1 and its company at 18 us were costed, W:0,5 and wsb were not, though both had passed the transposes on SP's queue, and the term for this wait was thus nothing. The part on the w_sp queue looked only at its end, where 0 was right: its reader sS:1,1 starts at 175.57, the last load is issued by 170.4, and gM:3 has no wait.

*Tail* (-0.25, -0.35 to +0.1): the failed step with the largest price, 1.3 to 2.1 us alone. The eviction was right to 0.01 us. What was left out is that the second part's bank gives PE a later last wait, and that something of 3.8 us on PE hangs on this wait. The price of +0.1 for two stores hindering each other bounded the wrong thing. The short rows, to which the chances give 0.05, did not decide: that rows of 384 B cost more than rows of 896 was assumed, and no run shows it; with the same 384-byte rows in free banks the time was that of before. A loss of 0.3 us would lie within that interval (0.9970 to 1.0019), though; the store of 48 KB landed in 2.34 us there, the whole-row store of 112 KB in 2.29.

*Start* (0, -0.25 to 0): in the mean not refuted, since the memset alone is 1.0009 (0.9993 to 1.0025); but the bound of 0 above was wrong for a single execution, where an idle stretch ahead of X:0 goes with a stretch at half clock (0.50 for 3.41 us, behind 1.10 of idling) that costs 1.1 us. The profiled execution that the prediction read was one without it.

*wM:15* (-0.26): right, and 0.42 in PE's own spacing. *gM:1* (-0.24): 0.29 won; a rest of 0.13 is left, since the last z2n tile comes at 139.7, some 137.1 with PE's lateness of 2.6 there taken off, and not near 136. Another 0.17, at P:0,0,7 (150.83 before), was won that no wait had shown.

*ScalarE between the gelus* (+0.13): 0.04. zG:1 ended at 84.78, zM:2 started at 84.92 with 0.16 of the weight load idle, close behind the bank. *gr:1*: 0, right. *qM:4*: 0.6 stayed, right.

Without the two failed steps the sum is +0.04 - 0.42 - 0.29 - 0.17 = -0.84, against -0.52 forecast; the runs without the two losses gave -0.3 to -0.4 in the median and -0.8 with the head covered.
